# Windowed attention and a feed-forward block in one kernel: another order of the first loads and masks, and a shorter flag

## The chip, the cores and the metric

The kernel runs on one core of a Trainium2 chip. The core has five engines with a program each: PE (TensorE, matrix products), DVE (VectorE), ACT (ScalarE), POOL (GpSimd) and SP (SyncE, which here issues every DMA). They wait for each other by semaphores alone. The metric is the device time of one execution in microseconds (us); the median of three runs of the kernel before is 794.26 us.

## What is computed

```python
scores = scale * np.matmul(q, k.transpose(0, 1, 3, 2))      # q, k, v: 4 x 8 x 768 x 64, float32
is_global = pos[None, :] < int(n_global)                    # n_global = 8, n_local = 96 (int64 inputs)
is_local = (rel >= 0) & (rel < int(n_local))                # rel = query position - key position
dist = np.where(is_global & ~is_local, float(n_local), np.abs(rel))
scores = np.where(is_global | is_local, scores - slopes * dist, -1000000000.0)
a = softmax(scores)                                         # with 1e-9 added to the sum
x = (a @ v), transposed and reshaped to 3072 x 512
h = x @ w_in                                                # 512 x 2048, float64
P = a0 + a1 * h + a2 * h * h + a3 * h * h * h               # moe_a
Q = 1.0 + |b0| * |h| + |b1| * h * h                         # moe_b
out = ((P / (Q + 1e-06)) @ w_out).astype(np.float32)        # 2048 x 512, float64
```

A query of tile i (128 rows) sees only keys of its own tile and of the one before, and the first eight keys.

## The kernel before

**Tiles and stages.** Work is cut into 96 *units* u: twelve chunks of 256 tokens, in each two row tiles of 128 and four pairs of heads. For a unit the kernel loads q, k and v (`st_load`, L127, one load for two units: `nat` holds q and k, `vt` holds v), splits q and k into a high and a low fp32r part (`st_split`, L368: a cast on DVE into tile `sp`, L369, and a subtraction on POOL, L370), transposes them on PE (`tk`, L378), copies them out on ACT (`qT`, `kT`, L392 to L397; two DMAs swap the halves of qT, L393 and L394), multiplies them (`s`, L408), adds the mask and takes the minimum on DVE (`pr`, L419), takes the exponential on ACT (L429), scales by the inverse sum on POOL (`norm`, L441), transposes on PE (`tp`, L462) and multiplies by v (`o`, L480). The result is kept as x, from chunk 1 on as a high part `xh` and a low part `xl` (L500).

The feed-forward block follows twelve steps later, in 96 steps f (eight for each chunk, two blocks of 128 hidden columns each): `h` (L250 in chunk 0, in plain fp32; L258 later, three fp32r products of high and low parts), the rational function in tiles `fu`, `fa`, `fs`, `q` and `g` on DVE, ACT and POOL (its last step in chunk 0 is L305 on DVE), and the second product `acc` (L329 in chunk 0, plain; L334 later). So fu6 is the activation of step 6, in chunk 0.

**Weights.** They arrive as float64 and are decoded to float32 on the chip, in 32 pieces of 128 x 512 (`decode`, L158 to L193): a load of 512 KB into a tile `r` (L163, three buffers), then four or five steps on ACT, POOL and DVE, by a table. Tiles `w1_a_b` are pieces of w_in, `w0_a` of w_out, with an f behind for the whole value and an l for the low part, which a subtraction on DVE or POOL makes (L210).

**Front.** `windowed` begins with the loads of units 0 and 2, the two counts (`ni`, four 32-bit integers on every partition, converted to `nf` on DVE, L513), and the coefficients (`load_coef`, L225). `window_masks` (L71) builds three 128 x 128 masks from nf: the one of the tile before (n = 0), the diagonal one (n = 1), a copy of the first, and from the diagonal one `mask0` for row tile 0, where the eight global columns are joined in. Behind everything in the program's text, `fl` and `fi` (L676 to L684) tell whether the counts lie in the range that this path serves (n_local from 1 to 121, n_global up to 8, high words zero); a second, general path runs only if they don't.

**What sets the order.** Nobody writes out the order of the engines' programs. Each piece of work gets a priority (1000 for each step t, plus an entry of the table `PRI_A` up to step 20 and of `PRI` later, L42 to L45), and a scheduler of the framework (`schedule_with_timeline_sim=True`) picks, with its own model of times, which ready instruction is next on each engine. A chip engine then runs its program strictly in that order. Buffers: `nat` and `vt` come from a pool with two and six buffers, `split` has one, the probability tile two.

Of the kernel before, what the change touches and what calls it, by code (L numbers as in the profile page):

```python
# [9 lines left out]
F32 = mybir.dt.float32  # L10
# [7 lines left out]
P = 128  # L18
G = 8
# [51 lines left out]
def window_masks(nc, scr, mask0, masks, nl, ng):  # L71

    rel, msk, key, g1 = scr
    for n, base in ((0, P), (1, 0)):
# [5 lines left out]
        if n:  # L80
            nc.gpsimd.affine_select(out=rel, in_=rel, pattern=[[-1, P]], base=0, channel_multiplier=1,
                                    compare_op=ALU.is_ge, fill=-BIG)
        nc.vector.tensor_tensor(out=m, in0=rel, in1=msk, op=ALU.add)

    nc.gpsimd.iota(key[:, 0:G], pattern=[[1, G]], base=0, channel_multiplier=0,
                   allow_small_or_imprecise_dtypes=True)
    nc.vector.tensor_scalar(out=g1[:, 0:G], in0=key[:, 0:G], scalar1=ng, scalar2=nl, op0=ALU.is_lt, op1=ALU.mult)
    nc.vector.tensor_scalar(out=g1[:, G:2 * G], in0=key[:, 0:G], scalar1=ng, scalar2=-BIG, op0=ALU.is_ge, op1=ALU.mult)
    nc.vector.tensor_tensor(out=masks[:, 0, 0:G], in0=g1[:, G:2 * G], in1=g1[:, 0:G], op=ALU.subtract)
    nc.vector.tensor_copy(out=mask0, in_=masks[:, 1, :])  # L90
    nc.vector.tensor_tensor(out=mask0[:, 0:G], in0=mask0[:, 0:G], in1=masks[:, 0, 0:G], op=ALU.max)
# [4 lines left out]
def tile_kernel(ctx: ExitStack, tc: tile.TileContext, q, k, v, n_global, n_local,  # L96
# [30 lines left out]
    def st_load(u):  # L127
# [6 lines left out]
        vt = pl.ldp.tile([P, 4, D], F32, tag="vt", name=f"vt{u}", bufs=6)  # L134
        nc.sync.dma_start(out=vt, in_=v[b, hs, r, :].rearrange("h s d -> s h d"))
        nat[u // 2] = n
        vts[u // 2] = vt
# [368 lines left out]
    def windowed():  # L506
        st_load(0)
        st_load(2)
        nc.sync.dma_start(out=ni[:, 0:2], in_=n_local.bitcast(I32).partition_broadcast(P))
        nc.sync.dma_start(out=ni[:, 2:4], in_=n_global.bitcast(I32).partition_broadcast(P))  # L510
        make_identity(nc, ident)
        nc.vector.tensor_copy(out=ident_r, in_=ident)
        nc.vector.tensor_copy(out=nf, in_=ni)  # L513
        load_coef()
        st_split(0)
        st_split(1)

        nl, ng = nf[:, 0:1], nf[:, 2:3]
        scr = tmp("scr").rearrange("p a (b w) -> p (a b) w", w=P)
        scr = [scr[:, x, :] for x in range(4)]  # L520
        window_masks(nc, scr, mask0, masks, nl, ng)

        base = tc.cur_priority
        for t in range(NU + LAG + F2):
# [151 lines left out]
    fl = const.tile([1, 8], F32, name="fl")  # L676
    fi = const.tile([1, 1], I32, name="fi")
    for n, (x, lo, hi) in enumerate(((0, 1.0, 121.0), (1, 0.0, 0.0), (2, 0.0, float(G)), (3, 0.0, 0.0))):
# [46 lines left out]
```

## Time and profile before

| | |
|---|---|
| median of three runs | 794.26 us (793.93 to 798.46) |
| the profiled execution | 792.2 us, its span 790.4 us |
| mean granted clock of PE | 0.992 |
| PE busy | 743.9 us (94%) |
| DVE busy | 599.6 us (76%) |
| ACT busy | 575.1 us (73%) |
| POOL busy | 533.3 us (67%) |
| busy in 0 to 160 us | PE 122.81, DVE 142.24 |

Busy times and the rows further below are of the profiled execution. A span covers everything from the first to the last recorded instruction. The profile puts every instruction at the line of the program that made it, with the tiles it writes and reads (numbers of buffers left out). Idle time stands in brackets with the instruction whose end let the engine go on. The share of the whole span says little about the first 160 us, in which the weights are loaded and decoded while attention starts.

### The profile page before, as it was taken

Reading aid. Unit: us, or ns where it says so; the run is one execution under the profiler, and the core shown is the slowest. Engines: PE = TensorE matmul, PEld = TensorE weight load, DVE = VectorE, ACT = ScalarE, POOL = GpSimd, SP = SyncE. Lnnn points to the kernel's source line nnn. Section 1 sums busy time; section 2 is a strip of 40 time slices with the busy share of each in tenths; the row PEclk is TensorE's granted clock in tenths of the full one; section 3 lists DMA queues with packets and bytes.
Section 4 is the critical chain, followed back from the end, with each engine's and each line's share of the span. In section 5 each row is a group of like instructions: output and inputs, shape, how many; then the busy total and the mean of one; then the engine's idle time right before and its main releaser. Section 6 shows DMA issues by size and latency. Waiting matters only on the chain.

```text
span 790.4 us, 15799 instructions
## 1 busy us (share of the span) xinstructions
PE 743.9 (94%) x5184; PEld 649.6 (82%) x5184; DVE 599.6 (76%) x1453; ACT 575.1 (73%) x1407; POOL 533.3 (67%) x572
## 2 busy tenths in 40 slices
PE   3688978899999999999999999999999999999995
PEld 2467647688998899999899999989999999988993
DVE  5889999987778676777776786777677786776664
ACT  4778677667887777777777777777877777766763
POOL 3868558979877667666667667666677777664440
PEclk9999999899999999999999999999999999999999
DMA  7785445212222233333332332333332332210000
GB/s 183 212 240 173 114 125 189 49 48 54 55 81 68 85 92 87 97 88 86 82 87 82 106 84 81 106 84 82 88 85 77 101 92 78 82 55 14 28 1 32
DMA packets 111932, 72.19 MB, mean 91 GB/s; under 512 B 82912, under 2 KB 97248, under 8 KB 111840
## 3 DMA queue, kind: packets, MB, share of 16 engines
q1 hardware_dynamic: 111840, 71.08, 32.0%
q8 instruction: 44, 0.72, 0.4%
q14 instruction: 48, 0.39, 0.2%
HBM read 35.92 MB, written 6.29 MB: 53 GB/s over the span
## 4 chain that ended last, share of the span: by engine, by line
PE 81%; DVE 6%; POOL 5%; DMA 4%; issue 2%; ACT 1%; SPq 0%; DVEq 0%; POOLq 0%; ACTq 0%
PE h L258 32%; PE acc L334 31%; PE o L480 5%; PE s L408 5%; PE tp L462 3%; PE tk L378 3%; DMA r<-in_moe_w_in_dram 2%; POOL pr L441 2%; PE h L250 1%; POOL sp L370 1%; DMA nat<-in_k_dram 1%; POOL fa L291 1%; DVE pr L419 1%; DVE fu L305 0%; DMA r<-in_moe_w_out_dram 0%
## 5 line engine op out<-in xcount | busy, mean ns | idle before, releaser
L334 PE MATMUL acc<-wout_h,g 128*128 128x512 f32 x704 | 242.8, 403 | 0.8 <-ACT g L313 0.8
L258 PE MATMUL h<-xh,win_h 128*128 128x256 f32 x704 | 205.4, 292 | 1.8 <-DVE fu L290 1.8
L441 POOL TENSOR_SCALAR pr<-pr,stats 128x256 f32<-128x256 f32 (+1 forms) x192 | 178.5, 940 | 39.2 <-issue 12.7
L258 PE MATMUL h<-xl,win_h 128*128 128x256 f32 x704 | 198.7, 282 | 0.0
L291 POOL TENSOR_TENSOR fa<-fa,fs 128x512 f32<-128x512 f32 x95 | 125.1, 1317 | 100.7 <-ACT fs L284 97.4
L334 PEld LDWEIGHTS acc<-wout_h,g 128*128 128x128 f32 x704 | 126.6, 188 | 21.8 <-ACT g L313 1.2
L258 PEld LDWEIGHTS h<-xh,win_h 128*128 128x128 f32 x704 | 133.3, 189 | 10.9 <-issue 6.2
L258 PEld LDWEIGHTS h<-xl,win_h 128*128 128x128 f32 x704 | 133.3, 189 | 2.3 <-issue 0.2
L429 ACT ACTIVATE pr<-pr,stats 128x256 f32<-128x256 f32 (+1 forms) x192 | 93.5, 492 | 53.5 <-DVE stats L419 53.4
L370 POOL TENSOR_TENSOR sp<-nat,sp 128x256 fp32r<-128x256 f32 x96 | 75.8, 790 | 73.5 <-DVE stats L432 41.0
L314 POOL TENSOR_TENSOR g<-fu,g 128x512 fp32r<-128x512 f32 x87 | 112.7, 1295 | 7.7 <-DVE fu L290 4.6
L282 ACT ACTIVATE fu<-h,coef 128x512 f32<-128x512 f32 (+1 forms) x97 | 75.4, 778 | 54.1 <-PE h L258 49.6
L303 DVE SCALAR_TENSOR_TENSOR fu<-fu,coef,q 128x512 f32<-128x512 f32 (+1 forms) x97 | 71.6, 738 | 36.2 <-ACT q L299 35.0
L298 ACT ACTIVATE fs<-fa,coef 128x512 f32<-128x512 f32 (+1 forms) x97 | 70.2, 724 | 30.3 <-POOL fa L291 27.9
L289 DVE TENSOR_TENSOR fu<-fu,h 128x512 f32<-128x512 f32 (+1 forms) x97 | 65.6, 677 | 16.9 <-ACT fs L284 14.9
L465 DVE COPY pT<-tp 128x512 f32<-128x512 f32 (+1 forms) x75 | 48.5, 646 | 35.7 <-PE tp L462 35.0
L369 DVE CAST sp<-nat 128x256 fp32r<-128x256 f32 x96 | 38.3, 399 | 46.7 <-PE tk L378 15.1
L290 DVE SCALAR_TENSOR_TENSOR fu<-fu,coef,h 128x512 f32<-128x512 f32 (+1 forms) x97 | 71.7, 739 | 2.5
L419 DVE CUSTOM_DVE_ANT_0 pr<-s,masks 128x256 f32<-128x256 f32 x160 | 61.4, 420 | 15.2 <-PE s L408 13.3
L408 PE MATMUL s<-kT,qT 128*128 128x256 f32 x384 | 70.5, 305 | 1.8 <-DMA qT<-qT 1.7
L304 DVE SCALAR_TENSOR_TENSOR q<-fa,coef,q 128x512 f32<-128x512 f32 (+1 forms) x97 | 72.1, 744 | 0.0
L408 PEld LDWEIGHTS s<-kT,qT 128*128 128x128 f32 x384 | 61.5, 203 | 9.0 <-DMA qT<-qT 1.9
(273 smaller groups left out, 1658.8 us busy)
## 6 DMA issues: line engine op xcount, KB each, us to landing
raw<-pr SPq DMA_DIRECT2D x58, 256.0 KB
qT<-qT SPq DMA_DIRECT2D x192, 64.0 KB
r<-in_moe_w_in_dram SPq DMA_DIRECT2D x16, 512.0 KB
r<-in_moe_w_out_dram SPq DMA_DIRECT2D x16, 512.0 KB
nat<-in_q_dram SPq DMA_DIRECT2D x48, 128.0 KB
nat<-in_k_dram SPq DMA_DIRECT2D x48, 128.0 KB
vt<-in_v_dram SPq DMA_DIRECT2D x48, 128.0 KB
out_dram<-o SPq DMA_DIRECT2D x24, 256.0 KB
```

Of the source, the lines that this page charges most:

```text
L258: nc.tensor.matmul(out=hps[f][:, y, :], lhsT=w[:, fs], rhs=x[:, ct, :], start=(n == 0), stop=(n == 3 * NCT - 1))
L282: nc.scalar.activation(out=u, in_=h, func=AF.Identity, scale=a3, bias=a2)
L290: nc.vector.scalar_tensor_tensor(out=u, in0=u, scalar=a1, in1=h, op0=ALU.add, op1=ALU.mult)
L291: side(f).tensor_tensor(out=a, in0=a, in1=s, op=ALU.add)
L303: nc.vector.scalar_tensor_tensor(out=u, in0=u, scalar=a0, in1=r, op0=ALU.add, op1=ALU.mult)
L304: nc.vector.scalar_tensor_tensor(out=r, in0=a, scalar=q1, in1=r, op0=ALU.add, op1=ALU.mult)
L314: side(f).tensor_tensor(out=g[:, 1, ys], in0=u, in1=g[:, 0, ys], op=ALU.subtract)
L334: nc.tensor.matmul(out=acc, lhsT=gs[f][:, z, y, ts], rhs=w, start=(ft == 0 and n == 0), stop=(ft == NFT - 1 and n == 2))
L370: nc.gpsimd.tensor_tensor(out=s[:, :, :, 1, :], in0=n, in1=s[:, :, :, 0, :], op=ALU.subtract)
L408: nc.tensor.matmul(out=s_ps[:, x], lhsT=qT[:, z, x, :], rhs=rhs, start=(z == 0), stop=(z == 1))
L429: nc.scalar.activation(out=d, in_=d, func=AF.Exp, scale=-1.0, bias=st[:, x:x + 1], accum_out=st[:, 2 + 2 * x:3 + 2 * x])
L441: nc.gpsimd.tensor_scalar(out=d, in0=d, scalar1=st[:, 6 + x:7 + x], scalar2=None, op0=ALU.mult)
```

## The change

Three things, all in the front or behind the end of the program's text. The loads of q and k are parted from the load of v (`st_load_v`, new): the two counts are loaded right behind q and k of unit 0, then q and k of unit 2, then v of both. `window_masks` makes the diagonal mask and mask0 first, with the global columns in a scratch tile `gm`, and the mask of the tile before second. The range test of the counts compares four numbers at once with a small table `lim`, which POOL fills, and takes a minimum: five DVE operations in place of fifteen. `load_coef` stands later in the text.

```diff
 def window_masks(nc, scr, mask0, masks, nl, ng):
     rel, msk, key, g1 = scr
-    for n, base in ((0, P), (1, 0)):
+    gm = g1[:, G:2 * G]
+    for n, base in ((1, 0), (0, P)):
         m = masks[:, n, :]
         nc.gpsimd.iota(rel, pattern=[[1, P]], base=-base, channel_multiplier=-1,
...
         nc.vector.tensor_tensor(out=m, in0=rel, in1=msk, op=ALU.add)
-
-    nc.gpsimd.iota(key[:, 0:G], pattern=[[1, G]], base=0, channel_multiplier=0,
-                   allow_small_or_imprecise_dtypes=True)
-    nc.vector.tensor_scalar(out=g1[:, 0:G], in0=key[:, 0:G], scalar1=ng, scalar2=nl, op0=ALU.is_lt, op1=ALU.mult)
-    nc.vector.tensor_scalar(out=g1[:, G:2 * G], in0=key[:, 0:G], scalar1=ng, scalar2=-BIG, op0=ALU.is_ge, op1=ALU.mult)
-    nc.vector.tensor_tensor(out=masks[:, 0, 0:G], in0=g1[:, G:2 * G], in1=g1[:, 0:G], op=ALU.subtract)
-    nc.vector.tensor_copy(out=mask0, in_=masks[:, 1, :])
-    nc.vector.tensor_tensor(out=mask0[:, 0:G], in0=mask0[:, 0:G], in1=masks[:, 0, 0:G], op=ALU.max)
+        if n == 0:
+            nc.vector.tensor_copy(out=masks[:, 0, 0:G], in_=gm)
+            continue
+
+        nc.gpsimd.iota(key[:, 0:G], pattern=[[1, G]], base=0, channel_multiplier=0,
+                       allow_small_or_imprecise_dtypes=True)
+        nc.vector.tensor_scalar(out=g1[:, 0:G], in0=key[:, 0:G], scalar1=ng, scalar2=nl, op0=ALU.is_lt, op1=ALU.mult)
+        nc.vector.tensor_scalar(out=gm, in0=key[:, 0:G], scalar1=ng, scalar2=-BIG, op0=ALU.is_ge, op1=ALU.mult)
+        nc.vector.tensor_tensor(out=gm, in0=gm, in1=g1[:, 0:G], op=ALU.subtract)
+        nc.vector.tensor_copy(out=mask0, in_=m)
+        nc.vector.tensor_tensor(out=mask0[:, 0:G], in0=mask0[:, 0:G], in1=gm, op=ALU.max)
     nc.vector.tensor_copy(out=masks[:, 2, :], in_=masks[:, 0, :])
...
         nc.sync.dma_start(out=n[:, 1], in_=k[b, hs, r, :].rearrange("h s d -> s h d"))
-        vt = pl.ldp.tile([P, 4, D], F32, tag="vt", name=f"vt{u}", bufs=6)
-        nc.sync.dma_start(out=vt, in_=v[b, hs, r, :].rearrange("h s d -> s h d"))
         nat[u // 2] = n
-        vts[u // 2] = vt
+
+    def st_load_v(u):
+        c, t, p, b, i = unit(u)
+        vt = vts[u // 2] = pl.ldp.tile([P, 4, D], F32, tag="vt", name=f"vt{u}", bufs=6)
+        nc.sync.dma_start(out=vt, in_=v[b, 2 * p:2 * p + 4, i * P:(i + 1) * P, :].rearrange("h s d -> s h d"))
...
     def windowed():
         st_load(0)
-        st_load(2)
         nc.sync.dma_start(out=ni[:, 0:2], in_=n_local.bitcast(I32).partition_broadcast(P))
         nc.sync.dma_start(out=ni[:, 2:4], in_=n_global.bitcast(I32).partition_broadcast(P))
+        st_load(2)
         make_identity(nc, ident)
         nc.vector.tensor_copy(out=ident_r, in_=ident)
+        st_split(0)
         nc.vector.tensor_copy(out=nf, in_=ni)
-        load_coef()
-        st_split(0)
-        st_split(1)
-
         nl, ng = nf[:, 0:1], nf[:, 2:3]
         scr = tmp("scr").rearrange("p a (b w) -> p (a b) w", w=P)
         scr = [scr[:, x, :] for x in range(4)]
+        st_split(1)
         window_masks(nc, scr, mask0, masks, nl, ng)
+        st_load_v(0)
+        st_load_v(2)
+        load_coef()
...
             if t % 2 == 0:
                 on("load", st_load, t + 4)
+                on("load", st_load_v, t + 4)
...
-    fl = const.tile([1, 8], F32, name="fl")
+    fl = const.tile([1, 4], F32, name="fl")
     fi = const.tile([1, 1], I32, name="fi")
-    for n, (x, lo, hi) in enumerate(((0, 1.0, 121.0), (1, 0.0, 0.0), (2, 0.0, float(G)), (3, 0.0, 0.0))):
-        nc.vector.tensor_scalar(out=fl[:, 4:5], in0=nf[0:1, x:x + 1], scalar1=lo, scalar2=None, op0=ALU.is_ge)
-        nc.vector.tensor_scalar(out=fl[:, 5:6], in0=nf[0:1, x:x + 1], scalar1=hi, scalar2=None, op0=ALU.is_le)
-        nc.vector.tensor_tensor(out=fl[:, n:n + 1], in0=fl[:, 4:5], in1=fl[:, 5:6], op=ALU.mult)
-    nc.vector.tensor_tensor(out=fl[:, 4:6], in0=fl[:, 0:2], in1=fl[:, 2:4], op=ALU.mult)
-    nc.vector.tensor_tensor(out=fl[:, 6:7], in0=fl[:, 4:5], in1=fl[:, 5:6], op=ALU.mult)
-    nc.vector.tensor_copy(out=fi, in_=fl[:, 6:7])
+    lim = const.tile([1, 2, 4], F32, name="lim")
+    nc.gpsimd.memset(lim, 0.0)
+    for x, w, val in ((0, 0, 1.0), (1, 0, 121.0), (1, 2, float(G))):
+        nc.gpsimd.memset(lim[:, x, w:w + 1], val)
+    nc.vector.tensor_tensor(out=fl, in0=nf[0:1], in1=lim[:, 0], op=ALU.is_ge)
+    nc.vector.tensor_tensor(out=lim[:, 0], in0=nf[0:1], in1=lim[:, 1], op=ALU.is_le)
+    nc.vector.tensor_tensor(out=fl, in0=fl, in1=lim[:, 0], op=ALU.mult)
+    nc.vector.tensor_reduce(out=lim[:, 1, 0:1], in_=fl, op=ALU.min, axis=mybir.AxisListType.X)
+    nc.vector.tensor_copy(out=fi, in_=lim[:, 1, 0:1])
```

Since the order is the scheduler's, the change moves instructions on all engines up to about unit 24, where both orders are the same again. In the changed program a line is four to ten numbers further down (L369 becomes L375, L329 becomes L335). Three places follow.

*First place, the front.* SP's queue from its first DMA, before:

```order
L132 DMA nat0_95<-in_q_dram 128x4x64
L133 DMA nat0_95<-in_k_dram 128x4x64
L135 DMA vt0_98<-in_v_dram 128x4x64
L132 DMA nat2_100<-in_q_dram 128x4x64
L133 DMA nat2_100<-in_k_dram 128x4x64
L135 DMA vt2_103<-in_v_dram 128x4x64
L509 DMA ni_72<-in_n_local_dram 128x2
L510 DMA ni_72<-in_n_global_dram 128x2
```
and after:

```order
L136 DMA nat0_95<-in_q_dram 128x4x64
L137 DMA nat0_95<-in_k_dram 128x4x64
L514 DMA ni_72<-in_n_local_dram 128x2
L515 DMA ni_72<-in_n_global_dram 128x2
L136 DMA nat2_100<-in_q_dram 128x4x64
L137 DMA nat2_100<-in_k_dram 128x4x64
L143 DMA vt0_135<-in_v_dram 128x4x64
L143 DMA vt2_137<-in_v_dram 128x4x64
```
The counts have gone from places seven and eight to three and four, and v of units 0 and 2 to the end.

DVE from the cast of sp0 on, before (scr are the masks' scratch tiles, rt and coef the coefficients'):

```order
L369 CAST sp0_126<-nat0_95 128x4x64
L369 CAST sp1_129<-nat0_95 128x4x64
L513 CAST nf_73<-ni_72 128x4
L78 TENSOR_SCALAR scr_132<-scr_132,nf_73 128x128
L87 TENSOR_SCALAR scr_132<-scr_132,nf_73 128x8
L234 TENSOR_SCALAR rt_117<-rt_117 128x1
L239 TENSOR_SCALAR rt_117<-rt_117 128x1
L88 TENSOR_SCALAR scr_132<-scr_132,nf_73 128x8
L679 TENSOR_SCALAR fl_9983<-nf_73 1x1
L79 TENSOR_SCALAR scr_132<-scr_132 128x128
L369 CAST sp2_195<-nat2_100 128x4x64
```
and after, from the cast of sp0 (fl and lim are the flag's):

```order
L375 CAST sp0_108<-nat0_95 128x4x64
L520 CAST nf_73<-ni_72 128x4
L79 TENSOR_SCALAR scr_112<-scr_112,nf_73 128x128
L91 TENSOR_SCALAR scr_112<-scr_112,nf_73 128x8
L92 TENSOR_SCALAR scr_112<-scr_112,nf_73 128x8
L690 TENSOR_TENSOR fl_9984<-nf_73,lim_9986 1x4
L80 TENSOR_SCALAR scr_112<-scr_112 128x128
L93 TENSOR_TENSOR scr_112<-scr_112 128x8
L691 TENSOR_TENSOR lim_9986<-nf_73,lim_9986 1x4
```
DVE after, from the eighth row behind nf up to the cast of sp1:

```order
L84 TENSOR_TENSOR masks_71<-scr_112 128x128
L692 TENSOR_TENSOR fl_9984<-fl_9984,lim_9986 1x4
L94 COPY mask0_70<-masks_71 128x128
L693 TENSOR_REDUCE lim_9986<-fl_9984 1x1
L375 CAST sp1_113<-nat0_95 128x4x64
```
Before, the cast of sp1 stood directly behind that of sp0 and ahead of nf. After, nf and eleven operations for masks and flag stand ahead of it.

*Second place, ACT at the first weight.* The weight's first two steps (L185 and L189 before, L191 and L195 after) and the exponentials of unit 0 (L429, L435), before:

```order
L397 COPY kG_67<-tk2_215 128x16
L185 ACTIVATE w1_2_0f_168<-r1_2_0_169 128x512
L189 ACTIVATE r1_2_0_169<-r1_2_0_169 128x512
L429 ACTIVATE pr0_208,stats_65<-pr0_208,stats_65 128x128 x2
L171 ACTIVATE w1_3_0f_175<-r1_3_0_176 128x512
```
and after:

```order
L435 ACTIVATE pr0_209,stats_65<-pr0_209,stats_65 128x128
L191 ACTIVATE w1_2_0f_169<-r1_2_0_170 128x512
L195 ACTIVATE r1_2_0_170<-r1_2_0_170 128x512
L435 ACTIVATE pr0_209,stats_65<-pr0_209,stats_65 128x128
L177 ACTIVATE w1_3_0f_176<-r1_3_0_177 128x512
```
One of the two exponentials has gone ahead of the weight's steps.

*Third place, the accumulation of fu6.* PE, before (from the last products of h9; acc is written by L329):

```order
L258 MATMUL h9_1556<-xh1_854,w1_3_0l_1230 128x256
L462 MATMUL tp18_1634<-ident_68,pr18_1442 128x128 x2
L408 MATMUL s20_1654<-kT_66,qT20_1467 128x256 x4
L329 MATMUL acc0_0_963<-w0_12f_1314,fu6_1291 128x512
L329 MATMUL acc0_0_963<-w0_13f_1321,fu6_1291 128x512
L329 MATMUL acc0_1_973<-w0_12f_1314,fu6_1291 128x512
L329 MATMUL acc0_1_973<-w0_13f_1321,fu6_1291 128x512
L462 MATMUL tp18_1634<-ident_68,pr18_1442 128x128 x2
L378 MATMUL tk22_1679<-ident_r_69,sp22_1594 128x128 x4
L462 MATMUL tp19_1732<-ident_68,pr19_1549 128x128 x2
L408 MATMUL s21_1761<-kT_66,qT21_1584 128x256 x4
L462 MATMUL tp19_1732<-ident_68,pr19_1549 128x128 x2
```
and after (acc is written by L335):

```order
L486 MATMUL o7_1370<-pT15_1311,vt10_378 64x128
L468 MATMUL tp16_1414<-ident_68,pr16_1257 128x128 x2
L414 MATMUL s18_1437<-kT_66,qT18_1274 128x256 x4
L468 MATMUL tp16_1414<-ident_68,pr16_1257 128x128 x2
L264 MATMUL h8_1450<-xh1_855,win_h_59 128x256
L335 MATMUL acc0_0_964<-w0_12f_1315,fu6_1292 128x512
L335 MATMUL acc0_0_964<-w0_13f_1322,fu6_1292 128x512
L335 MATMUL acc0_1_974<-w0_12f_1315,fu6_1292 128x512
L335 MATMUL acc0_1_974<-w0_13f_1322,fu6_1292 128x512
L264 MATMUL h9_1557<-xh1_855,win_h_59 128x256
L264 MATMUL h9_1557<-xl1_856,win_h_59 128x256
L264 MATMUL h9_1557<-xh1_855,w1_0_0l_1234 128x256
```
The accumulation of fu6 stood behind h8, h9, tp18 and s20. It now stands behind s18 and within h8, ahead of h9. DVE, which makes fu6, before (from its polynomial steps on; ISA rows are the score pass):

```order
L303 SCALAR_TENSOR_TENSOR fu6_1291<-fu6_1291,coef_64,q6_1390 128x512
L304 SCALAR_TENSOR_TENSOR q6_1390<-fa6_1292,coef_64,q6_1390 128x512
L419 ISA pr19_1549,stats_65<-s19_1543,masks_71 128x256
L419 ISA stats_65 128x1
L419 ISA pr19_1549,stats_65<-s19_1543,masks_71 128x256
L419 ISA stats_65 128x1
L369 CAST sp22_1594<-nat22_1245 128x4x64
L190 SCALAR_TENSOR_TENSOR r0_15_1337<-r0_15_1337 128x512
L305 SCALAR_TENSOR_TENSOR fu6_1291<-q6_1390,fu6_1291 128x512
```
and after:

```order
L309 SCALAR_TENSOR_TENSOR fu6_1292<-fu6_1292,coef_64,q6_1391 128x512
L310 SCALAR_TENSOR_TENSOR q6_1391<-fa6_1293,coef_64,q6_1391 128x512
L438 TENSOR_REDUCE stats_65<-stats_65 128x2
L295 TENSOR_TENSOR fu7_1400<-fu7_1400,h7_1360 128x512
L216 TENSOR_TENSOR w1_3_1l_1423<-w1_3_1f_592,win_h_59 128x512
L311 SCALAR_TENSOR_TENSOR fu6_1292<-q6_1391,fu6_1292 128x512
```
The score pass of pr19, the cast of sp22 and a decode step are gone from between, and a step of fu7 and a subtraction w1_3_1l have come in.

## Rows read from the trace of the kernel before

**Rows 1.** Windows: start:end, length, busy us (instructions) per engine, PEclk, DMA share, GB/s
```profile
60.00:160.00 100.00, 86.99 (x460) 63.05 (x459) 96.59 (x215) 73.76 (x176) 74.83 (x69) 0.95 0.44 128
160.00:770.00 610.00, 610.00 (x4495) 550.26 (x4494) 449.05 (x1064) 456.87 (x1099) 419.68 (x451) 1.00 0.27 76
```

**Rows 2.** Timeline of SP's queue (start, us, what was issued)
```profile
4.51 0.43 SPq L510 DMA_DIRECT2D ni<-in_n_global_dram  x1
...
7.33 0.45 SPq L132 DMA_DIRECT2D nat<-in_q_dram  x1
...
8.95 1.06 SPq L163 DMA_DIRECT2D r<-in_moe_w_in_dram  x2
...
16.23 0.58 SPq L163 DMA_DIRECT2D r<-in_moe_w_in_dram  x1
```

**Rows 3.** Timeline of DVE at the front (in brackets: idle before, and its releaser)
```profile
4.19 0.29 DVE L369 CAST sp<-nat 128x256 fp32r<-128x256 f32 x1 [2.39 <-DMA nat<-in_k_dram]
6.20 0.29 DVE L369 CAST sp<-nat 128x256 fp32r<-128x256 f32 x1 [1.72 <-PE tk L378]
8.02 0.17 DVE L513 CAST nf<-ni 128x4 f32<-128x4 int32 x1 [1.52 <-DMA ni<-in_n_global_dram]
...
14.21 0.29 DVE L419 CUSTOM_DVE_ANT_0 pr<-s,mask 128x128 f32<-128x128 f32 x1
```

**Rows 4.** Groups of DVE's instructions from 0 to 16 us (count, busy us, mean ns)
```profile
L681 DVE TENSOR_TENSOR fl<-fl 1x1 f32<-1x1 f32 x4 | 1.2, 295 | 0.0
...
L679 DVE TENSOR_SCALAR fl<-nf 1x1 f32<-1x1 f32 x4 | 0.5, 136 | 0.0
```

**Rows 5.** Timelines of POOL and of ACT at the front
```profile
6.57 0.72 POOL L370 TENSOR_TENSOR sp<-nat,sp 128x256 fp32r<-128x256 f32 x1 [1.28 <-DVE sp L369]
...
15.50 0.39 ACT L429 ACTIVATE pr<-pr,stats 128x128 f32<-128x128 f32 x1
```

**Rows 6.** Chain of waits from 8 to 21 us (start, us, what)
```profile
8.95 5.01 DMA r<-in_moe_w_in_dram
...
13.98 0.68 ACT w_0f L185
14.66 0.57 ACT r L189
...
16.23 4.26 DMA r<-in_moe_w_in_dram
```

**Rows 7.** Timeline of PE at five places
```profile
23.79 0.48 PE L462 MATMUL tp<-ident,pr 128*128 128x128 f32 x1 [3.26 <-POOL pr L441]
...
134.83 0.36 PE L258 MATMUL h<-xh,win_h 128*128 128x256 f32 x1
...
143.36 1.12 PE L329 MATMUL acc<-w_12f,fu 128*128 128x512 f32 x2
...
146.04 1.02 PE L329 MATMUL acc<-w_13f,fu 128*128 128x512 f32 x2
...
150.88 0.69 PE L462 MATMUL tp<-ident,pr 128*128 128x128 f32 x2 [3.31 <-POOL pr L441]
```

**Rows 8.** Timelines of DVE (around fu6) and of POOL (the tile PE waits for)
```profile
140.89 0.42 DVE L419 CUSTOM_DVE_ANT_0 pr<-s,masks 128x256 f32<-128x256 f32 x1
...
142.03 0.68 DVE L190 SCALAR_TENSOR_TENSOR r<-r 128x512 int32<-128x512 int32 x1
142.63 0.68 DVE L305 SCALAR_TENSOR_TENSOR fu<-q,fu 128x512 f32<-128x512 f32 x1
...
149.47 2.56 POOL L441 TENSOR_SCALAR pr<-pr,stats 128x256 f32<-128x256 f32 x2
```

**Rows 9.** Windows with the granted clock (PEclk), columns as in group 1
```profile
25.00:30.00 5.00, 4.37 (x22) 3.03 (x21) 4.89 (x14) 3.66 (x12) 2.36 (x4) 1.00 0.86 206
150.90:157.20 6.30, 6.28 (x29) 5.88 (x30) 6.30 (x17) 3.92 (x12) 6.01 (x5) 0.52 0.28 64
157.20:161.00 3.80, 3.80 (x13) 1.89 (x13) 3.40 (x9) 2.28 (x5) 2.53 (x3) 1.00 0.00 0
```
## The prediction

> **What bounds the kernel now.** I read the busy time by stage first [rows 1]. From 160 to 770 us PE is busy for all of 610.00 us, so nothing at the start can shorten that part. From 60 to 160 it is DVE that is full, 96.59 of 100 us, while PE works 86.99. So only the stretch before 160 can give or take time, and what counts is when PE enters its unbroken run. Its last long wait ends at 150.88 [rows 7]: 3.31 us, for a probability tile that POOL scales (L441, 149.47 [rows 8]).
>
> Next I read the queues at the front. SP issues the loads one after another; the first weight's load is issued at 8.95, behind nat4's at 7.33 [rows 2], which waits until POOL has read nat0 (6.57 + 0.72 us [rows 5]). The chain of waits then runs over that weight: 5.01 us of DMA, 0.68 and 0.57 on ACT, and soon 4.26 us of DMA for the next weight [rows 6]. So the start of the decode stage hangs on the cast of sp1 on DVE, sp1 on POOL, nat4's load and the weight's load, in this order, and the masks and the flag hang beside it.
>
> **The change part by part.** The sum is made on the profiled execution, 792.2 us; the median of the runs shown is 794.26, so 2.06 is added at the end.
>
> 1. *Flag.* Fifteen DVE operations become five. Four L679 cost 0.5 us, four L681 1.2 [rows 4]; the four L680 and the last three are of L679's kind and size, 0.14 each, so together 2.7. Five of 0.14 are 0.7. DVE saves 2.0 us, all of it before 16 us, where the chain waits 5.01 us for the first weight [rows 6]. The four memsets on POOL have no row of before; the nearest POOL row at the front is 0.72 us for 128x256 [rows 5], so they cost between 0 and 2.9 us, and four writes of at most eight numbers lie near the lower end, while POOL waits for DVE there. Value 0 (bounds -2.0 and 0).
>
> 2. *Counts loaded earlier, mask of tile 0 first.* The two loads of ni move up four places: only q and k of unit 0 are ahead of them, and the second is issued at about 2.3, as the fourth of issues of some 0.5 us. Now it takes 3.51 us from its issue (4.51 [rows 2]) to the use (8.02 [rows 3]); nf can then begin between 4.5, behind the cast of sp0 (4.19 [rows 3]), and 5.8. I take 5.4. The first probability tile has its mask before 13, where it now starts at 14.21 [rows 3]. But ACT is in between: in the new order the weight's first two steps (13.98 and 14.66 [rows 6]) stand between the two exponentials of pr0, so the second comes at about 15.2 instead of 15.50 [rows 5]. Gain 0 to 0.3; value -0.3.
>
> 3. *sp1 behind the masks.* The DVE queue now has nf and eleven mask and flag operations ahead of the cast of sp1. At 0.12 each (a little under L679's 0.136 [rows 4], since neighbours overlap) they take 1.4 us, so the cast comes at 6.8 in place of 6.20 [rows 3]. Queued behind it are POOL's half of sp1, nat4's load, and on SP the first weight: all 0.6 us later. Bounds 0 and, if nf starts no earlier than at 8.02, +3.3 (rival C). Value +0.6.
>
> 4. *V last.* SP has as many loads as before; v of units 0 and 2 changes place with the counts, and vt6 goes ahead of nat6, which waits at its place for POOL. A value load is not read until the first o; the slot it gives up, 0.5 us like the other issues of rows 2, can bring the load at 16.23 forward by that much. Bounds -0.5 and 0; value -0.3. Together 2, 3 and 4 are 0, with ends of -0.8 and +0.6.
>
> The Trainium skill, page "DMA: Bandwidth & Descriptors", section "Anatomy of one DMA — SWDGE (gpsimd) path", gives one transfer a fixed cost of about 2.0 us that does not shrink with its size. By it the counts would be there at about 4.3 (an estimate from that page), step 3 would cost nothing and the sum would be 0.6 lower. The 3.51 us of [rows 2, 3], for a few bytes behind larger loads, speak against that here, and the measurement decides.
>
> 5. *The decode stage in another order.* The scheduler orders all engines anew up to about unit 24, so the front's edit moves work at 130 to 160 us too. What matters is the last plain product of PE but one before its full run, the accumulation of fu6 (L329, 143.36 to 146.90 [rows 7]). DVE finishes fu6 at 142.63 + 0.68 = 143.3 [rows 8]. In the new order these stand behind it instead of ahead: the score pass of pr19, the cast of sp22 and a decode step (1.74 from 140.89 to 142.63 [rows 8]); the same of pr18 and sp21 (1.14, from 140.89 to 142.03); a polynomial step, 0.7 like L305, and a split of half that size, 0.3. One subtraction of L305's size, w1_3_1l, stands ahead: fu6 is ready 3.9 - 0.7 = 3.2 us sooner, at 140.1. On PE, however, its accumulation stands much further forward: most of h8, all of h9, tk20, tp17, s19, tk21, o8, half of tp18 and s20 are now behind it. From 134.83 on that is 143.36 - 134.83 = 8.5 us [rows 7]; with tk20 and tp17, which ran before 134.83 (0.9), and less the part of h8 that stays ahead (0.8), 8.6. PE would be there at 134.8 and waits 5.3 us for DVE. This new wait takes the place of the one at 150.88, since the tile PE waited for there has another 9 us of PE work ahead of it in the new order.
> From 140.1 on: the accumulation 3.5, the moved work 8.6, then what PE did between 146.90 and 161.00 without waits and at full clock: 150.88 - 3.31 - 146.90 = 0.7, then 6.28 x 0.52 = 3.3, then 3.80 [rows 7, 9]. That is 140.1 + 3.5 + 8.6 + 7.8 = 160.0 where 161.0 stood: -1.0. Now the clock: behind the wait of 3.31 us the granted clock was 0.52 for 6.30 us [rows 9], about the lower of the two levels (1.2 GHz for 2.4), which cost 6.28 x 0.48 = 3.0 us. If it falls in the same way behind the new wait, the same point comes at 163.0: +2.0. After 3.26 us without work, at 23.79, it was 1.00 [rows 7, 9]; after 3.31 it fell. The new wait would be longer than both, but DVE, a little ahead or late, can cut it to either. I take the middle, +0.5 (ends -1.0 and +2.0).
>
> The Trainium skill, page "TensorE: Matmul & The Clock Gate", section "HAM oscillation — how this bites in real kernels", says that a burst of matmuls behind a long wait for data starts at the lower clock again, and that each such wait pays anew. By it the upper end holds, +2.0; the trace agrees at 150.88.
>
> Sum: 792.2 + 0 + 0 + 0.5 = 792.7; on the level of the median 794.8.
>
> **Rivals.** *B, faster: no wait at fu6.* If DVE has fu6 ready by 134.8, PE works through: the old 3.31 us of idle time and the 3.0 us of half clock are both gone, and 794.26 - 6.3 = 788.0. For it: POOL's share of fu6, which stood behind two probability tiles, now stands ahead of them. Against it: DVE is full from 60 on [rows 1], and it would have to be 5.3 us further along than its order says.
> *C, slower: the counts land late.* If the loads around them hold them back as now, nf starts at 8.02, the cast of sp1 at 9.5 instead of 6.20, and nat4 and the first weight go out 3.3 us later. As DVE has little slack behind 60 us [rows 1], this comes through: 794.26 + 0.5 + 3.3 = 798.1 (796.6 to 799.6 with the ends of step 5). It decides from an nf later than about 5.8. For it: the 3.51 us. Against it: four large loads fewer are ahead.
> *D: the front is worth what it saves.* If DVE's 2.0 us at the start were on the path, the time would be 792.8; the wait of 5.01 us beside them speaks against it. It lies inside the forecast's own range.
>
> **How the numbers follow.** Forecast with D: 0.55, own range 792.0 to 797.0. B 0.18, C 0.20, and 0.07 for waits of the new order that these sums don't show (0.03 below 786.3, 0.04 above 802.2). The range from 788.0 to 800.0 takes in the forecast, half of B and most of C; it leaves out 0.09 + 0.03 + 0.07. A difference under about 1% (786.3 to 802.2) can't be told from no change by runs like these. Of B and of C, 0.01 each could lie beyond that bound: faster 0.04, same 0.91, slower 0.05.
>
> **What the profile after would show.** nf between 4.5 and 5.8, the cast of sp1 near 6.8, the first weight's issue near 9.5: right for 2 and 3. nf near 8: C. The first exponential of pr0 ahead of 13.98, the second near 15: right for 2. At fu6's accumulation a wait of PE of 4 to 6 us that DVE ends, near 140: right for 5; none: B. A granted clock near 0.5 for some 6 us behind it: the upper end. PE's full run beginning far from 160, or a long wait for POOL or a DMA after 140, would make the prediction wrong.

## The result: 0.57% slower, and the profile after

The changed kernel takes 798.17 us (median of 20 runs, 796.33 to 800.86), the kernel before in the same session 793.93 (20 runs, 791.54 to 798.46). The ratio is 1.0057, 95% interval [1.0044, 1.0069]: 4.2 us more. That lies within the bound of 1% and inside the range of 788.0 to 800.0, but above the forecast's own range (792.0 to 797.0), clear of no change, and 3.4 us above the point forecast. The profiled execution of after took 799.25 us (span 797.4); that of before 792.2 (span 790.4), so these two profiles are 7.0 us apart, more than the medians. One execution of the kernel e11 below (1026.97 us, mean granted clock 0.671) is left out of its median and ratio.

The stages first (stretch, its length, busy time and count of PE, PEld, DVE, ACT, POOL, then granted clock, DMA share, GB/s), after:

```profile
60.00:160.00 100.00, 88.53 (x445) 62.92 (x442) 93.76 (x204) 68.67 (x163) 70.40 (x67) 0.91 0.45 129
160.00:770.00 610.00, 606.41 (x4485) 548.00 (x4484) 450.57 (x1077) 456.95 (x1108) 420.69 (x453) 1.00 0.28 77
```

Against [rows 1]: PE is 1.54 us busier between 60 and 160, at a granted clock of 0.91 instead of 0.95. And the stretch from 160 on, where PE was busy for all of 610.00 us, now has 3.59 us in which it stands still. That stretch was left out of the prediction as one that cannot change.

The front, by SP's queue, DVE and ACT in order of time (start, duration, engine, line, operation, tiles; in brackets the idle time ahead and who ended it), after:

```profile
2.32 0.43 SPq L515 DMA_DIRECT2D ni<-in_n_global_dram  x1
...
8.91 0.39 SPq L136 DMA_DIRECT2D nat<-in_q_dram  x1
...
10.45 1.06 SPq L169 DMA_DIRECT2D r<-in_moe_w_in_dram  x2
...
17.37 0.35 SPq L169 DMA_DIRECT2D r<-in_moe_w_in_dram  x1
...
3.96 0.29 DVE L375 CAST sp<-nat 128x256 fp32r<-128x256 f32 x1 [2.15 <-DMA nat<-in_k_dram]
5.96 0.17 DVE L520 CAST nf<-ni 128x4 f32<-128x4 int32 x1 [1.71 <-DMA ni<-in_n_global_dram]
...
7.67 0.30 DVE L375 CAST sp<-nat 128x256 fp32r<-128x256 f32 x1
...
13.58 0.29 DVE L425 CUSTOM_DVE_ANT_0 pr<-s,mask 128x128 f32<-128x128 f32 x1 [1.51 <-PE s L414]
...
14.23 0.43 ACT L435 ACTIVATE pr<-pr,stats 128x128 f32<-128x128 f32 x1
...
15.62 0.67 ACT L191 ACTIVATE w_0f<-r 128x512 f32<-128x512 f32 x1 [0.87 <-DMA r<-in_moe_w_in_dram]
...
16.74 0.39 ACT L435 ACTIVATE pr<-pr,stats 128x128 f32<-128x128 f32 x1
```

The counts are used at 5.96 (8.02 before [rows 3]), the cast of sp1 comes at 7.67 (6.20 before), nat4's load at 8.91 (7.33) and the first weight's at 10.45 (8.95 [rows 2]). So the front's own chain is 1.5 us later than before.

Then the place where the forecast put a new wait, PE at the accumulation of fu6, and DVE's last step of fu6, after:

```profile
143.40 0.38 PE L468 MATMUL tp<-ident,pr 128*128 128x128 f32 x2
144.19 0.38 PE L264 MATMUL h<-xh,win_h 128*128 128x256 f32 x1 [0.40 <-ACT xh L505]
144.44 1.12 PE L335 MATMUL acc<-w_12f,fu 128*128 128x512 f32 x2
...
143.70 0.69 DVE L311 SCALAR_TENSOR_TENSOR fu<-q,fu 128x512 f32<-128x512 f32 x1
```

There is no wait at this accumulation: DVE finishes fu6 at 144.39 and PE comes at 144.44. PE's long waits are elsewhere, after (the waits of more than a microsecond behind 60 us, and all of them behind 160):

```profile
73.08 1.09 PE L468 MATMUL tp<-ident,pr 128*128 128x128 f32 x4 [3.62 <-ACT pT L471]
...
77.68 5.81 PE L256 MATMUL h<-x,w_1f 128*128 128x256 f32 x16 [2.66 <-DVE fu L296]
...
130.66 0.53 PE L384 MATMUL tk<-ident_r,sp 128*128 128x128 f32 x4 [1.78 <-POOL sp L376]
...
133.48 3.50 PE L335 MATMUL acc<-w_10f,fu 128*128 128x512 f32 x4 [1.82 <-DVE w_10f L184]
...
179.21 0.39 PE L264 MATMUL h<-xh,win_h 128*128 128x256 f32 x1 [0.58 <-DVE fu L296]
...
188.47 0.50 PE L384 MATMUL tk<-ident_r,sp 128*128 128x128 f32 x4 [0.50 <-DVE stats L438]
...
189.70 0.39 PE L264 MATMUL h<-xh,win_h 128*128 128x256 f32 x1 [0.72 <-DVE fu L296]
...
221.35 0.38 PE L264 MATMUL h<-xh,win_h 128*128 128x256 f32 x1 [1.79 <-DVE fu L296]
```

The last four add up to the 3.59 us. In three of them DVE's second step on an h tile (L296) is late, and PE cannot begin the next product; in the fourth, of 0.50 us, PE's transposes wait, by the profile for a reduction on DVE (L438). The 3.31 us for POOL at 150.88 [rows 7] is gone. Two stretches of after show the clock around the first two of these waits and behind the last (columns as for the stages):

```profile
73.00:79.00 6.00, 3.26 (x11) 2.82 (x12) 6.00 (x13) 5.62 (x14) 3.52 (x5) 0.50 0.53 154
...
221.40:225.00 3.60, 3.60 (x18) 3.50 (x19) 2.54 (x5) 1.84 (x3) 3.60 (x4) 0.57 0.10 22
```

Both stand near the lower level, 1.2 GHz, which before had near 151 [rows 9].

### The profile page after: what moved, and what is told of

Its sections match the earlier page's. It is cut to its first block, busy times and chain, and to the rows that moved or that the text cites. A ratio compares the mean times of both kernels' runs of the same rounds, so it can differ in the third digit from the quotient of the medians.

```text
span 797.4 us, 15773 instructions
## 1 busy us (share of the span) xinstructions
PE 745.8 (94%) x5184; PEld 651.7 (82%) x5184; DVE 599.3 (75%) x1444; ACT 573.3 (72%) x1407; POOL 531.8 (67%) x576
## 4 chain that ended last, share of the span: by engine, by line
PE 77%; DVE 10%; DMA 5%; issue 3%; ACT 2%; POOL 2%; SPq 1%; DVEq 0%; POOLq 0%; ACTq 0%
PE h L264 30%; PE acc L340 29%; PE o L486 5%; PE s L414 4%; PE tk L384 3%; PE tp L468 3%; DMA r<-in_moe_w_in_dram 2%; PE h L256 2%; DMA qT<-qT 1%; DMA r<-in_moe_w_out_dram 1%; PE acc L335 1%; DVE q L310 1%; POOL pr L447 1%; DVE fu L311 1%; DVE pr L425 1%
## 5 line engine op out<-in xcount | busy, mean ns | idle before, releaser
L435 ACT ACTIVATE pr<-pr,stats 128x256 f32<-128x256 f32 (+1 forms) x192 | 93.2, 489 | 58.1 <-DVE stats L425 58.1
L376 POOL TENSOR_TENSOR sp<-nat,sp 128x256 fp32r<-128x256 f32 x96 | 73.1, 762 | 66.1 <-DVE stats L438 32.5
L309 DVE SCALAR_TENSOR_TENSOR fu<-fu,coef,q 128x512 f32<-128x512 f32 (+1 forms) x97 | 71.6, 738 | 35.8 <-ACT q L305 33.9
L375 DVE CAST sp<-nat 128x256 fp32r<-128x256 f32 x96 | 37.1, 386 | 50.1 <-PE tk L384 17.4
L296 DVE SCALAR_TENSOR_TENSOR fu<-fu,coef,h 128x512 f32<-128x512 f32 (+1 forms) x97 | 71.8, 740 | 2.6
L425 DVE CUSTOM_DVE_ANT_0 pr<-s,masks 128x256 f32<-128x256 f32 x160 | 61.3, 419 | 12.7 <-PE s L414 11.3
```

Source lines behind the costliest of these rows:

```text
L296: nc.vector.scalar_tensor_tensor(out=u, in0=u, scalar=a1, in1=h, op0=ALU.add, op1=ALU.mult)
L309: nc.vector.scalar_tensor_tensor(out=u, in0=u, scalar=a0, in1=r, op0=ALU.add, op1=ALU.mult)
L376: nc.gpsimd.tensor_tensor(out=s[:, :, :, 1, :], in0=n, in1=s[:, :, :, 0, :], op=ALU.subtract)
L435: nc.scalar.activation(out=d, in_=d, func=AF.Exp, scale=-1.0, bias=st[:, x:x + 1], accum_out=st[:, 2 + 2 * x:3 + 2 * x])
```

## Experiments

One question runs through them: does the time come from what the edit does (the front 1.5 us late, the new place of the masks), or from the order into which the scheduler puts all engines because of it? Called *order 1* is PE's order of before, *order 2* that of after; where an order is named, PE's instructions stand in it word for word, unless it says otherwise. Each kernel is compared with executions of before from its own session.

### The parts alone

**e1_flag**: before with the five-operation flag of the diff, nothing else.

> The kernel before with the flag in five operations alone; PE's and ACT's instruction order is that of before, word for word. Theory F (front: the first weight is issued later, 10.45 us after the change for 8.95 before) and theory O (order: the new order of the decode stage costs the time) both expect no change: 793.9 us, within 1 us, first weight issued at 8.95. The rival that DVE's 2.0 us at the front are on the path expects 791.9.

Measured: 794.25 us against 794.46, ratio 0.998 [0.9964, 0.9996]; order 1. The flag costs nothing. A gain of up to 0.4% stands in the interval, which takes in the 791.9 us of the rival, though the medians are 0.2 us apart. It does not come through the front: the first weight goes out at 9.30, not at 8.95 as expected, and no earlier than before.

**e7_mask**: before with only the mask function of the diff.

> The kernel before with the order of the masks alone; PE's and ACT's order is that of before, word for word. All theories expect 794 us, within 1 us: pr0 starts earlier (near 13.5 for 14.21), but the two exponentials stay behind the first weight's steps on ACT.

Measured: 793.39 against 793.75, ratio 0.9998 [0.998, 1.0017]; order 1. The order of the masks alone is worth nothing that can be told, at most 0.2% either way.

**e2_loads**: before with only the loads changed; the counts' cast and load_coef stay where they were in the text.

```diff
+    def st_load_v(u):
...
         st_load(0)
-        st_load(2)
         nc.sync.dma_start(out=ni[:, 0:2], ...
         nc.sync.dma_start(out=ni[:, 2:4], ...
+        st_load(2)
+        st_load_v(0)
+        st_load_v(2)
```

> The kernel before with the load order alone (counts second, V last); masks and flag as before. The PE order comes out as that of the changed kernel, word for word, and the cast of sp1 has nf and 11 operations ahead of it. Theories F and O both expect the whole loss, 797 to 799 us, first weight issued near 10.4. If the masks' or the flag's new form carry a part of it, less: 794 to 796.

Measured: 798.47 against 794.46, ratio 1.0049 [1.0032, 1.0067]. It has nearly the whole loss, but two things go together in it: a late front (cast of sp1 at 7.36, first weight at 10.13) and order 2.

### The late front against the new order

**e3_new_order_early_cast**: after, with masks and flag held until POOL has made its half of sp1, so that the cast of sp1 comes first again. Three small copies on POOL do it.

```diff
         st_split(1)
+        nc.gpsimd.tensor_copy(out=scr[0][:, 0:1], in_=sp[1][:, 0, 0, 1, 0:1])
+        nc.gpsimd.tensor_copy(out=scr[2][:, 0:1], in_=sp[1][:, 0, 0, 1, 0:1])
+        held1.append(sp[1])
         window_masks(nc, scr, mask0, masks, nl, ng)
...
+    nc.gpsimd.tensor_copy(out=lim[:, 0, 0:1], in_=held1[0][0:1, 0, 0, 1, 0:1])
     nc.gpsimd.memset(lim, 0.0)
```

> The changed kernel with masks and flag held back until POOL has made its part of sp1 (three small POOL copies more), so that the cast of sp1 has only nf ahead of it. PE's order is that of the changed kernel, word for word. nf at 5.96, the cast of sp1 at 6.2, the first weight issued near 9.0. Theory F expects the loss to go: 793 to 795 us. Theory O expects it to stay: 797 to 799.

**e4_old_order_late_cast**: before with the loads of the diff and the masks held by one such copy, which leaves the cast of sp1 late, but brings order 1 back.

```diff
         scr = [scr[:, x, :] for x in range(4)]
+        nc.gpsimd.tensor_copy(out=scr[0][:, 0:1], in_=sp[1][:, 0, 0, 1, 0:1])
         window_masks(nc, scr, mask0, masks, nl, ng)
```

> The kernel before with the new load order (counts second, V last) and the masks, not the flag, held back until POOL has made its part of sp1 (one small POOL copy more). PE's and ACT's order come out as those of before, word for word, but the cast of sp1 has nf and 9 operations ahead of it: at about 7.3, the first weight issued near 10. Theory F expects the loss to come with it: 797 to 799 us. Theory O expects 793 to 795.

Measured: e3 798.0 against 794.46, ratio 1.0044 [1.0027, 1.0061]; e4 794.67, ratio 1.0002 [0.9983, 1.0021]. The two fronts, first e3, then e4 (DVE's cast of sp1 and SP's first weight):

```profile
6.25 0.29 DVE L375 CAST sp<-nat 128x256 fp32r<-128x256 f32 x1
...
9.31 1.08 SPq L169 DMA_DIRECT2D r<-in_moe_w_in_dram  x2
```

```profile
7.33 0.29 DVE L371 CAST sp<-nat 128x256 fp32r<-128x256 f32 x1
...
9.99 1.09 SPq L165 DMA_DIRECT2D r<-in_moe_w_in_dram  x2
```

An early front in order 2 loses 3.5 us; a front late by 1.0 us in order 1 loses nothing. The delay is absorbed, at least up to that 1.0 us (after's own is 1.5), and the loss follows the order.

**e9_flag_and_mask** and **e10_old_order_loads_flag** make the cross complete. e9 is before with flag and masks, the old loads kept. e10 is after with the old mask function and the three copies of e3: new loads and new flag.

> The kernel before with the flag and the masks of the change, not its loads. SP's front and DVE's up to the cast of sp1 are those of before (sp1 cast at 6.2 to 6.5, first weight at 8.95 to 9.3), but PE's order comes out as that of the changed kernel, word for word, while flag alone and mask alone left it as it was. Theory S (the new order costs it, wherever it comes from; about 4 us more idle time of DVE before 160 us): 797 to 799 us. If the late first weight or the new loads are needed for the loss: 793 to 794.5, as flag alone and mask alone.

> The changed kernel with the masks of before, masks and flag held back until POOL has made its part of sp1 (three small POOL copies more). New loads and new flag, the cast of sp1 right behind nf at 6.2, and PE's and ACT's order come out as those of before, word for word. Theory S: 792 to 794.5 us, no loss. If the new loads (counts second, V last) cost the time: 797 to 799.

Measured: e9 797.16 against 793.63, ratio 1.004 [1.0022, 1.0058], order 2; e10 793.66, ratio 0.9995 [0.9972, 1.0018], order 1. Flag and masks, each harmless alone and in order 1, flip the order together, and the loss is there without one load moved. The loads, which had the loss when they came alone, have none in order 1. The first weight goes out at 9.10 in e9 and at 9.16 in e10, so this pair has one front and two orders. Its stages (columns as above), first e9, then e10:

```profile
0.00:60.00 60.00, 32.18 (x169) 25.43 (x170) 45.02 (x145) 36.26 (x118) 35.94 (x55) 0.99 0.74 202
60.00:160.00 100.00, 91.21 (x467) 65.47 (x467) 93.51 (x205) 71.42 (x166) 73.47 (x69) 0.92 0.47 133
65.00:80.00 15.00, 9.58 (x44) 7.68 (x43) 11.43 (x25) 11.53 (x26) 6.82 (x7) 0.75 0.51 153
170.00:225.00 55.00, 51.41 (x365) 45.84 (x364) 43.08 (x111) 38.49 (x105) 46.89 (x50) 0.97 0.23 51
```

```profile
0.00:60.00 60.00, 33.43 (x178) 25.88 (x179) 43.73 (x147) 36.43 (x118) 38.90 (x61) 1.00 0.77 210
60.00:160.00 100.00, 87.27 (x457) 62.94 (x456) 95.56 (x209) 71.84 (x174) 71.19 (x66) 0.93 0.45 128
65.00:80.00 15.00, 12.12 (x78) 10.25 (x77) 14.69 (x36) 14.15 (x35) 11.77 (x10) 1.00 0.55 168
170.00:225.00 55.00, 55.00 (x404) 49.45 (x403) 44.01 (x109) 42.16 (x108) 45.55 (x46) 1.00 0.23 55
```

In this pair order 2 loses at two places behind 60: between 65 and 80 (2.5 us less PE work, at a clock of 0.75 instead of 1.00), and between 170 and 225 (3.59 us of idle time, clock 0.97 instead of 1.00). The low clock at the first place is not order 2's alone: e1, in order 1, has 0.77 there. In between order 2 regains: over the whole of 60 to 160 PE is idle for 8.8 us in e9, 12.7 in e10; 3.33 us of that are the long wait for POOL (near 151 in before, at 153.65 in e10), which order 2 does not have. The second place is the one that stays.

### Inside the order

In after, ACT takes the first three steps of fu0 at 69.98, behind two decode steps of weights (66.83, which had waited 3.40 us for its load, and 69.41); in before they stood ahead of these decode steps, at 61.44. First after, then before:

```profile
66.83 0.68 ACT L177 ACTIVATE w_5f<-r 128x512 f32<-128x512 f32 x1 [3.40 <-DMA r<-in_moe_w_out_dram]
...
69.41 0.66 ACT L177 ACTIVATE w_2f<-r 128x512 f32<-128x512 f32 x1 [1.40 <-DMA r<-in_moe_w_in_dram]
69.98 0.77 ACT L288 ACTIVATE fu<-h,coef 128x512 f32<-128x512 f32 x1
```

```profile
61.44 0.78 ACT L282 ACTIVATE fu<-h,coef 128x512 f32<-128x512 f32 x1 [0.34 <-PE h L250]
```

One theory was that this alone makes the waits at 73 and 78 and all that follows. **e5_fu0_ahead_of_w102** puts fu0's steps ahead of the second decode step, **e6_fu0_ahead_of_both** ahead of both (there the key is (0, 5)). Two entries of the decode table go from step 11 to step 12, and a copy of one column ties the weight's tile to fu0.

```diff
-... 11: [(0, 0), (0, 2), (1, 4)], 12:
-          [(0, 3), (0, 4)], ...
+... 11: [(0, 0)], 12:
+          [(0, 2), (1, 4), (0, 3), (0, 4)], ...
...
+        if key in ((1, 0, 2),):
+            nc.scalar.copy(out=dst[:, 0:1], in_=ew[0]["s"][:, 0, 0:1])
```

> The changed kernel, but on ACT the three activations of fu0 stand ahead of the first decode step of w1_0_2 (a small ACT copy of fu0's result into that weight's tile makes the scheduler keep them ahead; the copy is overwritten by the step). The rest of the order is nearly that of the changed kernel (26 rows of 5184 on PE differ). Theory A (what the new order costs is made at 66 to 73 us, where ACT waits for weights w0_5 and w1_0_2 with fu0 queued behind): fu0 starts 2.0 us earlier, at 68 instead of 69.98, PE's wait of 3.62 us shrinks by as much: 796 us. Theory S (the cost is spread over the whole new order, and this wait hides others): 797.5 to 799, no change.

> As the kernel before this one, but fu0 stands ahead of the first decode step of w0_5 and of that of w1_0_2, as in the kernel before the change. More of the order differs from the changed kernel's (346 rows on PE). Theory A: fu0 starts at about 66, the wait near 73 goes, 794 to 795 us. Theory S: 797 to 799.

Measured: e5 800.78 against 793.75, ratio 1.0085 [1.0061, 1.0109]; e6 799.39, ratio 1.0073 [1.0052, 1.0093]. Neither is faster than after, and both lie above what either theory expected. e5 keeps order 2 but for 26 rows on PE; e6 has another. In e5 fu0 starts at 67.46, and PE's wait near 73 falls to 2.01 us, without any gain in time. PE's long waits in e6 between 60 and 90:

```profile
70.06 5.38 PE L258 MATMUL h<-x,w_1f 128*128 128x256 f32 x16 [3.56 <-DVE fu L298]
...
82.97 6.32 PE L258 MATMUL h<-x,w_1f 128*128 128x256 f32 x16 [5.30 <-DVE fu L298]
```

ACT's share came sooner (66.48), and PE then waited longer for DVE's. The theory falls as the sufficient cause; what it moves is the wait's place.

**e8_weight_first**: before with the first two weights' loads given the priority of the first loads, so that the first goes out near 6.5.

```diff
-                tc.cur_priority = base + 1000 * t + pri["dec"] + 50 * n
+                tc.cur_priority = base + (50 if t == 0 else 1000 * t + pri["dec"] + 50 * n)
```

> The kernel before with the first weight's load ahead of nat4's on SP (a lower number in the priority of step 0's weights): issued near 6.6 in place of 8.95, the second weight behind nat4. The order of the decode stage is a third one. If the start of the first weight set the time, with whatever order, 791 to 792 us; if the order of the decode stage does, anything from 791 to 799, with the wait at fu0 as the sign: none there, and it is near 793.

Measured: 796.64 against 793.75, ratio 1.0044 [1.0018, 1.0071], in an order of its own. The first weight went out at 6.41 and not at 8.95: in this order a start of the chain 2.5 us sooner does not pay for the order's own idle time (45.5 us up to 250 in the table below, in an execution 4.3 us above this kernel's median).

**e11_third_order**: after, with the counts' cast on POOL behind its half of sp1 instead of on DVE. It has all of the change in it but for the engine of this cast, an early cast of sp1 (6.12) and first weight (9.16), and a further order, far from both (554 rows of PE from before, 640 from after).

```diff
-        nc.vector.tensor_copy(out=nf, in_=ni)
...
         st_split(1)
+        nc.gpsimd.tensor_copy(out=nf[:, 0:1], in_=sp[1][:, 0, 0, 1, 0:1])
+        nc.gpsimd.tensor_copy(out=nf, in_=ni)
```

> The changed kernel with nf made by POOL behind its part of sp1, so that sp1's cast on DVE stands right behind that of sp0. The scheduler makes a further order of it (554 rows on PE differ from before, 640 from the changed kernel). If only the changed kernel's own order is bad: 793 to 795. If the order of before is better than what the scheduler makes on its own of a changed front: 796 to 800, with 42 us or more of idle time on PE up to 250 us.

Measured: 792.95 (nine executions) against 793.63, ratio 0.9993 [0.9974, 1.0013]. Its stages:

```profile
60.00:160.00 100.00, 89.75 (x489) 66.20 (x488) 94.25 (x210) 74.28 (x176) 72.45 (x69) 0.94 0.46 130
160.00:770.00 610.00, 607.98 (x4482) 547.51 (x4481) 446.84 (x1069) 456.18 (x1101) 421.64 (x452) 1.00 0.27 75
```

The whole change without its loss: so no part of it is slow by itself. This version also has 2.0 us of idle time behind 160, but less ahead of it. It beats after by about 5 us, each set against its own session, and before by nothing that can be told.

### All of them by order

Idle time of PE in one profiled execution each, which is the length of a stage less PE's busy time in it (us; from the view by stage; no kernel has any from 250 to 770):

| order | kernel | 0 to 60 | 60 to 160 | 160 to 250 | sum | ratio to before |
|---|---|---|---|---|---|---|
| 1 | before | 24.2 | 13.0 | 0.0 | 37.2 | 1 |
| 1 | e1 | 25.7 | 14.0 | 0.0 | 39.7 | 0.998 |
| 1 | e7 | 26.7 | 13.3 | 0.0 | 39.9 | 0.9998 |
| 1 | e4 | 26.0 | 11.0 | 0.0 | 37.0 | 1.0002 |
| 1 | e10 | 26.6 | 12.7 | 0.0 | 39.3 | 0.9995 |
| 2 | after | 26.9 | 11.5 | 3.6 | 42.0 | 1.0057 |
| 2 | e2 | 28.1 | 12.4 | 1.5 | 42.0 | 1.0049 |
| 2 | e3 | 28.0 | 11.3 | 3.6 | 42.9 | 1.0044 |
| 2 | e9 | 27.8 | 8.8 | 3.6 | 40.2 | 1.004 |
| other | e5 | 27.8 | 11.8 | 3.3 | 43.0 | 1.0085 |
| other | e6 | 28.7 | 16.0 | 2.1 | 46.8 | 1.0073 |
| other | e8 | 32.1 | 11.2 | 2.2 | 45.5 | 1.0044 |
| other | e11 | 25.3 | 10.3 | 2.0 | 37.6 | 0.9993 |

The five kernels in order 1 have ratios of 0.998 to 1.0002, the four in order 2 of 1.004 to 1.0057, whatever parts of the change they carry. The mean idle time is 38.6 us in order 1 and 41.8 in order 2: 3.2 of the 3.5 to 4.2 us. By stage order 2 has 1.9 us more up to 60, 1.8 less from 60 to 160, and 3.1 more from 160 to 250: what is lost between 65 and 80 has been regained by 160. These are single executions, which differ by up to 2.9 us within an order (e9's 40.2 is 0.3 above e7's 39.9), and some lie off their kernel's median (e8 took 800.94 us for 796.64, e7 791.04 for 793.39), so the sum supports the finding and does not measure it finely.

The clock goes the same way. Its mean over all executions of a kernel is 0.988 to 0.990 for every kernel in order 1 and 0.980 to 0.983 for every one in order 2; e5, e6 and e8, which lose as well, have 0.981 to 0.984, and e11 has 0.987. What that costs is not shown: PE's busy time in the profiles is on the mean 744.6 us in order 2 and 744.0 in order 1.

## Why the prediction held in size and missed in cause

*Flag (step 1, value 0).* Right as far as can be told: e1 loses nothing, and its interval also takes in the bound of -2.0.

*Counts and masks (step 2, -0.3).* The cast of the counts came at 5.96, a little past the bound of 5.8. The sum took it at 5.4; with four large loads fewer ahead, the counts were to land sooner after their issue. They did not: 3.51 us from issue to use before [rows 2, 3], 3.64 after (5.96 - 2.32). The Trainium skill, page "DMA: Bandwidth & Descriptors", section "Anatomy of one DMA — SWDGE (gpsimd) path", puts about 2.0 us of fixed cost on a transfer of that path, which POOL issues. These loads are issued by SP, so the prediction took its 4.3 from a figure for another path; both measurements are longer, and they decide here. The scores' first tile then waited for PE (1.51 us), not for its mask. The first exponential came at 14.23, not ahead of 13.98, and the second at 16.74 instead of 15.2, behind a weight that was itself late. So the gain of 0.3 did not come; e7 shows that the order of the masks is worth nothing either.

*sp1 behind the masks (step 3, +0.6).* The mechanism was there, the size was off: +1.5. The counts' 0.56 us add to eleven operations that took 1.71 us from 5.96 to 7.67 with nf, where 1.4 were reckoned. But e4 shows that a front late by 1.0 us costs nothing, so the term should have been near 0 in any case.

*V last (step 4, -0.3).* The next weight's load (the third; the first two go out together, x2) came at 17.37, 1.1 us later than before, while the first came 1.5 us later: 0.4 brought forward, as reckoned. In e4 the new loads gain nothing.

*The new order (step 5, +0.5).* This is the step that failed. It looked for the effect of the new order at one place, where fu6 was to be ready at 140.1 and PE there at 134.8. Both came near 144.4, since the sum took the starting times of before at 130 to 140 as those of after, although the same order had delayed PE long before: up to 144.44 PE had stood still for 38.4 us in after, against 33.9 up to 134.83 in before, and its clock from 60 on was 0.89, against 0.98. No wait stands there, and no fall of the clock (1.00 from 144 to 150): from this wait alone rival B would have come true. The new order's price was at places that the argument had not opened. Ahead of 160 there are the stretch up to 60 (26.9 us of idle time for 24.2) and that from 65 to 80, with waits of 3.62 and 2.66 us and a clock near 0.50 around them; the loss of the second is made up by 160. The other place is behind 160, 3.59 us, and there it was the opening premise that misled: "PE is busy for all of 610.00 us" [rows 1] says that nothing can be gained there, and was read as if nothing could be lost. Nor are the two orders the same from about unit 24 on, as the part on the change says: in the traces PE's rows of before and after (operation, tiles, sizes) last differ at 321.3 us of before, near unit 42, well behind these waits.

*The rivals.* The time fell on C's figure (798.1), and its condition was met by 0.16 us, but its cause is refuted: with order 1 a front late by 1.0 us costs nothing (e4), with order 2 the loss comes without it (e3, e9). So it is luck that the range, widened for C, held the time; the forecast's own range did not. B's wait did disappear, without its gain. D is neither seen nor excluded: with flag, new loads and an early front, e10 stands at 0.9995, but D's 792.8, 0.18% under before, lies in the intervals of e10 and of e1. The line of 0.07 for waits that the sums don't show had the right cause, but stood for times outside 786.3 to 802.2.

*What stays open.* Which exchange of places in order 2 makes DVE late for PE between 170 and 225 is not settled. Ahead of the wait at 221.35, DVE runs a cast of 1.19 us, three steps of another block and a score pass before L296, and had itself waited 0.8 to 0.9 us for ACT twice. The order of PE does not fix these waits by itself: e2, in order 2 as well, has 1.5 us behind 160 and not 3.6, with the same loss in time. Moving fu0's steps on ACT (e5, e6) changed where the waits are and did not remove them.

## What to carry to other kernels

Where a scheduler orders the engines, an edit of the first microseconds is two edits: what it does, and another order for everything up to the point where the orders meet again. Test them apart by building variants that carry the edit in the old order and the new order without the edit; here the order was worth 0.4 to 0.6%, and the edit in the old order nothing that could be told. And a stretch in which an engine is never idle says what cannot be gained there, not what cannot be lost.

## What the runs showed of the hardware

The length of one wait did not tell what the clock did behind it. Before, 3.26 us were followed by 1.00 and 3.31 by 0.52 [rows 7, 9]. In after, the wait of 1.79 us at 221.35 was followed by 0.57, although this wait was all the idle time that PE had had since 190 (29.61 us busy of 31.40, below), and one of 3.16 us was followed by 1.00 (PE's row, then the stretch behind it and that ahead of 221.40):

```profile
18.11 0.98 PE L414 MATMUL s<-kT,qT 128*128 128x256 f32 x3 [3.16 <-DMA qT<-qT]
```

```profile
18.20:21.00 2.80, 2.40 (x10) 1.81 (x11) 2.05 (x9) 1.87 (x9) 1.19 (x2) 1.00 0.99 263
...
190.00:221.40 31.40, 29.61 (x217) 26.39 (x215) 23.37 (x69) 23.93 (x65) 28.59 (x32) 1.00 0.24 53
```

The Trainium skill, page "TensorE: Matmul & The Clock Gate", section "HAM oscillation — how this bites in real kernels", has each burst behind a long wait for data start at the lower clock. The trace agrees at 73.08 (0.50 behind 3.62 us) and not at 18.11 (1.00 behind 3.16 us), and it shows the fall behind a much shorter wait at 221.35 (0.57 behind 1.79 us).
